# Weight conversions behind attention sums, the 64-token product in another bank, tile 0 loaded by three issuers

## The chip, the core and the metric

The kernel runs on one core of a Trainium2 chip. The metric is the device time of one execution, in microseconds (us); for the kernel before it is the median of three runs. One more execution was recorded by the hardware profiler, and all rows below are of that one.

## What is computed

A decaying attention (no softmax), two matrix layers with a product between them, and a mixture of 8 experts with a cap:

```python
B, H, S, D_ = q.shape                      # 8, 8, 576, 64
scores = 1.0 / np.sqrt(D_) * np.matmul(q, k.transpose(0, 1, 3, 2))
gamma = 1.0 - 2.0 ** (-5.0 - np.arange(H, dtype=np.float32))
rel = pos[:, None] - pos[None, :]
Dmat = np.where(rel >= 0, gamma[:, None, None] ** rel[None, :, :], 0.0)
x = np.matmul(scores * Dmat[None], v)      # -> 4608 tokens of 512
x = ((x @ w1) * (x @ w2) @ w3 @ w_out).astype(np.float32)   # 512 -> 1024 -> 1024 -> 512
logits = x @ w_gate                        # 8 experts
# (token, expert) pairs in falling order of logit: a token goes to the first
# expert that still has room (576 tokens each)
out[mask_e] = np.maximum(x[mask_e] @ w1[e], 0.0) @ w2[e]    # for each expert e
```

The weights w1, w2, w3 and w_out come as 64-bit floats, and the kernel makes 32-bit ones of them on the chip.

## The kernel before

**Attention.** The 4608 tokens are 36 tiles of 128; three tiles are a block of 384 (`TB`), and there are 12 blocks (`NB`). For a tile t, `att_load` loads q, k and v, `att_scale` scales q and k by the decay (L261, VectorE), `att_T` transposes them on TensorE (L274) and ScalarE copies the result out (L276). `att_P` multiplies k by v (L300), `att_QK` q by k (L283), `att_mask` applies the decay mask (L288, VectorE), `att_state` carries the running state on (L310, L312), and `att_AV` multiplies scores and state into two banks (L321, L329). `att_out` adds both: a copy on ScalarE (L337), the sum on VectorE (L343, two halves), its high part on ScalarE (L344) and its low part on GpSimd (L345). High and low part are the x on which the layers work. The generator `attention` issues these in the order seen below and yields a cost after each piece; `T(t + 2)` runs two tiles ahead. A half tile at the start of a sequence (in tiles 0, 4 and so on) has no state before it and so no sum.

**Precision.** Every product of the layers is three matrix products: high x high, high x low, low x high. So each weight is converted from 64 to 32 bits and split, in units of 128 x 512 (`conv`): an absolute value on ScalarE (L196), two one-operand and two two-operand steps on VectorE (L197, L198, L200, L202), the high part on ScalarE (L215), the low part on VectorE (L216). Units 0 to 15 are w1 and w2 by column blocks in turn (unit 8 and 9: w1 and w2 for f = 4), 16 to 23 w_out, from 24 on w3.

**Layers.** `ab(i)` computes (x @ w1) * (x @ w2) for block i: for each of 8 column blocks f one group of 12 products with w1 and one with w2 (L549), a copy by ScalarE (L556) and a multiplication by VectorE (L558). `ab(0)` calls for conversions `LEAD[f]` units ahead of the group at hand. `begin` lays the start: six attention steps merged with the first `LEAD[0]` units, then the first 8 groups of ab(0) merged with `2 * PER` attention steps by the ratio `RAT[1]`, then ab(0) and ab(1) in turn, two groups each (192 products in a row on TensorE), then w3's transposes (`w34_T`, L391) and the rest. w3 and w_out are multiplied into one matrix beforehand. What `merge` gives is a program order; from it a scheduler sets each engine's own queue, and an engine works its queue in order.

**Experts.** For expert e the output products are five groups (L1049): four of 128 tokens and one of 64 (o = 4). Each takes a bank by `mm_bank()`, of which there are two (p4, p5). The 128-token banks are copied out by ScalarE (L1055); the 64-token one needs a copy of one half (L1058) and VectorE's add of the other (L1059). GpSimd scatters the rows to the output (L1060). `HB` are the four half banks in which the first expert layer (L1027) is summed, named py. The order of this stage is planned from modelled times.

**Loads.** SP issues the loads in the order of `ORDER` ("q0 c0 k0 v0 ...": c are constants, w pairs of weight units).

Of the kernel before, what the change touches and what calls it, by code (L numbers as in the profile page):

```python
# [15 lines left out]
TB, NB = 384, 12  # L16
PT = 96
EARLY, LATE0 = 4, 8
LEAD = (3, 4, 4, 4, 4, 4, 4, 4)
LATE = 1.25  # L20
TRIPS = 8
ROUNDS = ((0, 6), (-4, 6), (-4, 6), (-4, 6), (-5, 6))
ORDER = "q0 c0 k0 v0 c1 q1 k1 w0 v1 w1 q2 k2 v2 w2 w3 c2"
Q0 = 10
RAT = (0.75, 0.45, 0.35, 0.36)


def shape_constants():
# [56 lines left out]
def build(ctx, tc, io):  # L85
# [44 lines left out]
    def mm_bank():  # L130
        return MM[nxt("mm", 2)]
# [52 lines left out]
    def conv(u):  # L184
        raw = raws.pop(u)
        lo, hi = raw[:, :, :, 0], raw[:, :, :, 1]
        if u[0] == "w3":
            b = 2048 + 512 * nxt("cv3", 2)
            ta = raw_t[:, b:b + 512]
        else:  # L190
            b = 512 * nxt("cv", 6)
            ta = tmp_t[:, b:b + 512]
        out = ta
        ta = ta.rearrange("p (k f) -> p k f", k=4)
        tb = hi.bitcast(F32)
        A.activation(ta, hi.bitcast(F32), AF.Abs)  # L196
        V.tensor_scalar(ta, ta, HIGH, LOW, op0=OP.min, op1=OP.max)  # L197
        V.tensor_scalar(ta.bitcast(I32), ta.bitcast(I32), 3, 0x3FFFFFF8,  # L198
                        op0=OP.logical_shift_left, op1=OP.bitwise_and)
        V.scalar_tensor_tensor(tb.bitcast(I32), hi, -1073741824, ta.bitcast(I32),  # L200
                               op0=OP.bitwise_and, op1=OP.bitwise_or)
        V.scalar_tensor_tensor(ta.bitcast(I32), lo, 29, tb.bitcast(I32),  # L202
                               op0=OP.logical_shift_right, op1=OP.bitwise_or)
        n, i, j = u
        if n == "w3":
            w3f[u] = out
            return
        hs, ls = SLOT(n)
        if n == "wo":
            hd, ld = hs[:, i, :], ls[:, i, :]  # L210
            fl = out
        else:
            hd, ld = (x[:, :, 128 * i:128 * i + 128] for x in (hs, ls))
            fl = ta
        A.activation(hd, fl, AF.Copy)  # L215
        V.tensor_tensor(ld, fl, hd.bitcast(F32), op=OP.subtract)  # L216
# [97 lines left out]
    def att_AV(t):  # L314
# [9 lines left out]
        for s in range(2):  # L324
            for a in range(2):
                for u, b in QUADS:
# [3 lines left out]
                              buf(t)[2][halves(u), 256 * s + 64 * c:256 * s + 64 * c + 64],  # L330
                              AM[s][halves(u), 64 * c:64 * c + 64], start=True, stop=True, skip_group_check=True)

    def att_out(t):
        j, o = divmod(t, 3)
        us = [u for u in range(2) if (2 * t + u) % 9]
# [2 lines left out]
        for u in range(2):  # L338
            xh, xl = (x[:, :, 128 * o + 64 * u:128 * o + 64 * u + 64] for x in XT[j % 2])
            po = PX[u][:, 0:256]  # L340
            if u in us:
                f = fk[u]
                V.tensor_tensor(f, po.rearrange("p (s a i) -> p s a i", a=2, s=2), f, op=OP.add)  # L343
                A.activation(xh.rearrange("p (s a) i -> p s a i", s=2), f, AF.Copy)  # L344
                G.tensor_tensor(xl.rearrange("p (s a) i -> p s a i", s=2), f,  # L345
                                xh.bitcast(F32).rearrange("p (s a) i -> p s a i", s=2), op=OP.subtract)
# [5 lines left out]
    def attention():  # L352
        def T(t):
            if t < NT:
                att_scale(t)
                att_T(t)
                if t != 2:
                    att_load(t + (3 if t < 2 else 2), (0,))
# [6 lines left out]
        yield 2500  # L365
        for t in range(NT):
            att_AV(t)
            if t + 1 < NT:
                att_P(t + 1)
                att_QK(t + 1)  # L370
                att_mask(t + 1)
            att_out(t)
            yield 2400
            if t + 1 < NT:
                att_state(t + 1)
            T(t + 2)
            att_load(t + 3, (1,))
            if t != 2:
                att_load(t + (3 if t < 2 else 2), (2,))
            yield 1400  # L380
# [633 lines left out]
    def expert(e):  # L1014
# [23 lines left out]
                yield 1500  # L1038
        vh, vl = (slot(i, 8) for i in pairs[(2 * e + 1) % 3])
        for o in (0, 1, 2, 3, 4) if e < E - 1 else (0, 4, 1, 2, 3):  # L1040
            p = mm_bank()
            for f in range(8):
                if o < 4:
                    s = slice(128 * o, 128 * o + 128)
# [65 lines left out]
    def begin():  # L1110
        merge(take(6), conv_some(LEAD[0]), RAT[0])
        a0, a1 = ab(0), ab(1)
        s = take(2 * PER)
        merge(take_from(a0, 8), s, RAT[1])
        drain(s)
        merge(turns(2, a0, take_from(a1, 8)), take(1), RAT[2])
# [16 lines left out]
    for c in ORDER.split():  # L1133
# [5 lines left out]
            load_pair(n)  # L1139
            nload[0] = n + 1  # L1140
        else:
            att_load(n, ("qkv".index(c[0]),))
    G.memset(wg, 0.0)
    SP.dma_start(wg[:, :, 0:8], io["wgate"].rearrange("(c p) e -> p c e", p=128))
    G.memset(WG, 0.0)
# [71 lines left out]
```

## Time and profile before

| what | us |
|---|---|
| median of three runs | 1303.81 (1303.66 to 1306.4) |
| the profiled execution | 1303.38 |
| its span, first to last instruction | 1301.6 |
| TensorE busy | 1256.4 (97%) |
| VectorE / ScalarE / GpSimd busy | 529.0 / 460.8 / 254.4 |

The mean granted clock of TensorE is .984 of its upper level over the span. TensorE is the busiest engine by far, but the share is a mean: the first slices of the span and the last one show less. The other engines are idle for more than half of the time, though not in every stretch. What an engine waits for is read from the waits, from the timeline around one place, and from its queue.

### The profile page before, as it was taken

The page shows a single profiled execution, that of the slowest core. Times are in us where ns is not written, and L with a number is a line of the kernel's source. Part 1 is how long each engine was busy: PE and PEld are TensorE (multiplying, and loading weights), DVE is VectorE, ACT ScalarE, POOL GpSimd, SP SyncE. Part 2 cuts the span into 40 slices and gives each one's busy share as a digit, 9 for nine tenths or more (in the row PEclk, how much of TensorE's full clock was granted, in tenths as well). Part 3 has the DMA queues.
Part 4 walks back from the last instruction along what each step waited for, and adds up shares of the span by engine and source line. Part 5 has one row for each costly group of instructions (what it writes and reads, how often), then busy time and mean ns, then how long its engine had stood idle before and what let it go on. Part 6 is the DMA issues. An engine that isn't in the chain of part 4 may idle for free. (4 is left out here: it accounts for less than half of the span.)

```text
span 1301.6 us, 27200 instructions
## 1 busy us (share of the span) xinstructions
PE 1256.4 (97%) x11416; PEld 1112.1 (85%) x11416; DVE 529.0 (41%) x1298; ACT 460.8 (35%) x989; POOL 254.4 (20%) x238
## 2 busy tenths in 40 slices
PE   5789999999999999999999999989999999999996
PEld 4678988889898989889899777778989989899885
DVE  6797544433231312212212555553533524335220
ACT  4443433343322222212221544333543534435221
POOL 1101211112211120201110734432120211211011
PEclk7799999999999999999999999999999999999999
DMA  9766444422312131424012312163533524435110
GB/s 243 221 163 198 133 131 134 127 64 61 83 34 74 25 83 25 131 87 134 10 49 93 114 45 98 42 190 119 154 121 114 157 67 150 140 96 153 47 39 29
DMA packets 156382, 136.00 MB, mean 104 GB/s; under 512 B 119264, under 2 KB 119520, under 8 KB 155232
## 3 DMA queue, kind: packets, MB, share of 16 engines
q1 hardware_dynamic: 150368, 115.35, 30.3%
q0 software_dynamic: 5888, 18.88, 4.6%
q8 instruction: 91, 1.49, 0.5%
q14 instruction: 35, 0.29, 0.1%
HBM read 107.19 MB, written 27.00 MB: 103 GB/s over the span
## 5 line engine op out<-in xcount | busy, mean ns | idle before, releaser
L549 PE MATMUL p<-x,ws 128*128 128x384 f32 x2304 | 424.1, 339 | 1.7 <-POOL x L345 0.9
L549 PEld LDWEIGHTS p<-x,ws 128*128 128x128 f32 x2304 | 398.2, 189 | 9.8 <-issue 3.9
L1049 PE MATMUL p<-ws,g 128*128 128x512 f32 x864 | 217.9, 394 | 1.9 <-DVE rs L1059 1.4
L1049 PEld LDWEIGHTS p<-ws,g 128*128 128x128 f32 x864 | 156.5, 188 | 31.6 <-DVE rs L1059 1.8
L904 PE MATMUL p<-ws,x 128*128 128x512 f32 x576 | 140.3, 398 | 0.0
L558 DVE TENSOR_TENSOR g<-p,ms 128x384 f32<-128x384 f32 x88 | 48.9, 556 | 183.1 <-PE p L549 180.2
L904 PEld LDWEIGHTS p<-ws,x 128*128 128x128 f32 x576 | 104.8, 189 | 20.6 <-issue 0.7
L941 DVE TENSOR_TENSOR ws<-x,ws 128x512 fp32r<-128x512 f32 x120 | 80.8, 690 | 100.6 <-ACT ws L940 92.7
L261 POOL TENSOR_TENSOR a<-a,cst 128x512 f32<-128x512 f32 x52 | 54.9, 1056 | 302.4 <-DMA a<-q 223.0
L940 ACT ACTIVATE ws<-x 128x512 fp32r<-128x512 f32 x128 | 78.2, 629 | 74.4 <-DMA x<-ew 57.8
L556 ACT ACTIVATE ms<-p 128x384 f32<-128x384 f32 x96 | 47.0, 489 | 151.4 <-PE p L549 149.6
L345 POOL TENSOR_TENSOR x<-a,x 128x256 fp32r<-128x256 f32 x64 | 49.4, 783 | 258.6 <-ACT x L344 258.6
L1060 POOL DMA_INDIRECT out<-rs,idx x40 | 40.0, 999 | 266.6 <-ACT g L1036 147.0
L601 PE MATMUL p<-ws,g 128*128 128x512 f32 x288 | 71.9, 398 | 0.0
L601 PEld LDWEIGHTS p<-ws,g 128*128 128x128 f32 x288 | 52.5, 188 | 13.4 <-issue 2.5
L1027 PE MATMUL p<-a,ws 128*128 128x320 f32 (+1 forms) x384 | 58.9, 301 | 0.5 <-ACT a L1010 0.5
L1036 ACT ACTIVATE g<-py 128x256 fp32r<-128x256 f32 x96 | 31.5, 328 | 75.1 <-PE py L1027 65.1
L1027 PE MATMUL p<-x,ws 128*128 128x320 f32 (+1 forms) x384 | 57.3, 297 | 0.3 <-DVE g L1037 0.3
L1027 PE MATMUL py<-a,ws 128*128 128x320 f32 (+1 forms) x384 | 57.0, 296 | 0.0
L1027 PEld LDWEIGHTS p<-a,ws 128*128 128x128 f32 x384 | 55.1, 193 | 2.1 <-ACT a L1010 0.6
L1027 PE MATMUL py<-x,ws 128*128 128x320 f32 (+1 forms) x384 | 56.4, 296 | 0.3 <-DVE g L1037 0.3
L1027 PEld LDWEIGHTS py<-x,ws 128*128 128x128 f32 x384 | 54.0, 189 | 2.6 <-DVE g L1037 0.7
(191 smaller groups left out, 1484.6 us busy)
## 6 DMA issues: line engine op xcount, KB each, us to landing
x<-ew SPq DMA_DIRECT2D x128, 256.0 KB
y_scratch<-ms SPq DMA_DIRECT2D x36, 256.0 KB
a<-k SPq DMA_DIRECT2D x64, 128.0 KB
ws<-w SPq DMA_DIRECT2D x8, 1024.0 KB
a<-q SPq DMA_DIRECT2D x62, 128.0 KB
a<-v SPq DMA_DIRECT2D x31, 256.0 KB
g_scratch<-g SPq DMA_DIRECT2D x8, 768.0 KB
g<-g_scratch SPq DMA_DIRECT2D x4, 1536.0 KB
```

What stands on the lines that cost most here:

```text
L261: (V if t < Q0 else G).tensor_tensor(xx, xx, tb_[:, :, None].to_broadcast([128, H, DH]), op=OP.mult)
L345: G.tensor_tensor(xl.rearrange("p (s a) i -> p s a i", s=2), f, xh.bitcast(F32).rearrange("p (s a) i -> p s a i", s=2), op=OP.subtract)
L549: PE.matmul(p[:, :TB], w[:, kk, fs], x[:, kk, :], start=(kk == 0 and j == 0), stop=(kk == 3 and j == 2))
L556: A.activation(a, p[:, :TB], AF.Copy)
L558: V.tensor_tensor(g[:, f, :], p[:, :TB], a, op=OP.mult)
L601: PE.matmul(p, x[:, f, ts], w[:, f, :], start=(f == 0 and j == 0), stop=(f == 7 and j == 2))
L904: PE.matmul(p, x[:, f, :], w[:, f, :], start=(f == 0 and j == 0), stop=(f == 7 and j == 2))
L940: A.activation(h, st, AF.Copy)
L941: low.tensor_tensor(lo[:, 512 * u:512 * u + 512], st, h.bitcast(F32), op=OP.subtract)
L1027: PE.matmul(p[:, :n], w[:, kk, fs], x[kk][:, ts], start=(kk == 0 and j == 0), stop=(kk == 3 and j == 2))
L1049: PE.matmul(p, x, w[:, f, :], start=(f == 0 and j == 0), stop=(f == 7 and j == len(ops) - 1))
L1060: st = G.indirect_dma_start(out=out, out_offset=bass.IndirectOffsetOnAxis(ap=idx[:n, 5 * e + o:5 * e + o + 1], axis=0), in_=ob[:n], in_off ...
```

## The change

`conv`: from the fourth unit on, VectorE's first step is issued only after the latest attention sum but one (and not before that of tile 2). `LEAD` falls from 4 to 2, so ab(0) calls for conversions two units ahead; `RAT[1]` rises from .45 to .9. `att_out` of tile 2 comes directly behind its `att_AV`; the scaling of tile 3 and 4 is issued after tile 2's sums, and tile 3's transposes behind that. In the expert stage the 64-token group takes one of the four half banks instead of p4 or p5. k0 is loaded by ScalarE's queue, v0 by GpSimd's, all else by SP's.

```diff
--- before.py
+++ after.py
@@ -1,4 +1,4 @@
-from contextlib import ExitStack
+from contextlib import ExitStack, nullcontext
 import numpy as np
 import concourse.bass as bass
 from concourse import mybir
@@ -16,13 +16,13 @@
 TB, NB = 384, 12
 PT = 96
 EARLY, LATE0 = 4, 8
-LEAD = (3, 4, 4, 4, 4, 4, 4, 4)
+LEAD = (3, 2, 2, 2, 2, 2, 2, 2)
 LATE = 1.25
 TRIPS = 8
 ROUNDS = ((0, 6), (-4, 6), (-4, 6), (-4, 6), (-5, 6))
 ORDER = "q0 c0 k0 v0 c1 q1 k1 w0 v1 w1 q2 k2 v2 w2 w3 c2"
 Q0 = 10
-RAT = (0.75, 0.45, 0.35, 0.36)
+RAT = (0.75, 0.9, 0.35, 0.36)
 
 
 def shape_constants():
@@ -194,7 +194,9 @@
         ta = ta.rearrange("p (k f) -> p k f", k=4)
         tb = hi.bitcast(F32)
         A.activation(ta, hi.bitcast(F32), AF.Abs)
-        V.tensor_scalar(ta, ta, HIGH, LOW, op0=OP.min, op1=OP.max)
+        behind = tc.issue_after(sums[max(2, max(sums) - 1)].ins) if u in units[3:] else nullcontext()
+        with behind:
+            V.tensor_scalar(ta, ta, HIGH, LOW, op0=OP.min, op1=OP.max)
         V.tensor_scalar(ta.bitcast(I32), ta.bitcast(I32), 3, 0x3FFFFFF8,
                         op0=OP.logical_shift_left, op1=OP.bitwise_and)
         V.scalar_tensor_tensor(tb.bitcast(I32), hi, -1073741824, ta.bitcast(I32),
@@ -330,6 +332,8 @@
                               buf(t)[2][halves(u), 256 * s + 64 * c:256 * s + 64 * c + 64],
                               AM[s][halves(u), 64 * c:64 * c + 64], start=True, stop=True, skip_group_check=True)
 
+    sums = {}
+
     def att_out(t):
         j, o = divmod(t, 3)
         us = [u for u in range(2) if (2 * t + u) % 9]
@@ -340,7 +344,7 @@
             po = PX[u][:, 0:256]
             if u in us:
                 f = fk[u]
-                V.tensor_tensor(f, po.rearrange("p (s a i) -> p s a i", a=2, s=2), f, op=OP.add)
+                sums[t] = V.tensor_tensor(f, po.rearrange("p (s a i) -> p s a i", a=2, s=2), f, op=OP.add)
                 A.activation(xh.rearrange("p (s a) i -> p s a i", s=2), f, AF.Copy)
                 G.tensor_tensor(xl.rearrange("p (s a) i -> p s a i", s=2), f,
                                 xh.bitcast(F32).rearrange("p (s a) i -> p s a i", s=2), op=OP.subtract)
@@ -352,7 +356,8 @@
     def attention():
         def T(t):
             if t < NT:
-                att_scale(t)
+                with tc.issue_after(sums[2].ins) if t == 4 else nullcontext():
+                    att_scale(t)
                 att_T(t)
                 if t != 2:
                     att_load(t + (3 if t < 2 else 2), (0,))
@@ -365,15 +370,24 @@
         yield 2500
         for t in range(NT):
             att_AV(t)
+            if t == 2:
+                att_out(t)
+                yield 1400
+                with tc.issue_after(sums[2].ins):
+                    att_scale(3)
+                att_T(3)
+                att_load(5, (0,))
             if t + 1 < NT:
                 att_P(t + 1)
                 att_QK(t + 1)
                 att_mask(t + 1)
-            att_out(t)
+            if t != 2:
+                att_out(t)
             yield 2400
             if t + 1 < NT:
                 att_state(t + 1)
-            T(t + 2)
+            if t != 1:
+                T(t + 2)
             att_load(t + 3, (1,))
             if t != 2:
                 att_load(t + (3 if t < 2 else 2), (2,))
@@ -1038,7 +1052,7 @@
                 yield 1500
         vh, vl = (slot(i, 8) for i in pairs[(2 * e + 1) % 3])
         for o in (0, 1, 2, 3, 4) if e < E - 1 else (0, 4, 1, 2, 3):
-            p = mm_bank()
+            p = mm_bank() if o < 4 else HB[nxt("hb", 4)]
             for f in range(8):
                 if o < 4:
                     s = slice(128 * o, 128 * o + 128)
@@ -1110,7 +1124,7 @@
     def begin():
         merge(take(6), conv_some(LEAD[0]), RAT[0])
         a0, a1 = ab(0), ab(1)
-        s = take(2 * PER)
+        s = take(2 * PER + 1)
         merge(take_from(a0, 8), s, RAT[1])
         drain(s)
         merge(turns(2, a0, take_from(a1, 8)), take(1), RAT[2])
@@ -1139,7 +1153,7 @@
             load_pair(n)
             nload[0] = n + 1
         else:
-            att_load(n, ("qkv".index(c[0]),))
+            att_load(n, ("qkv".index(c[0]),), A if c == "k0" else G if c == "v0" else SP)
     G.memset(wg, 0.0)
     SP.dma_start(wg[:, :, 0:8], io["wgate"].rearrange("(c p) e -> p c e", p=128))
     G.memset(WG, 0.0)

```

What this moves on the engines. In the rows below a name such as a1_10_73 is a region of memory with its place and use, and p0 to p5 and py are banks. The first place is VectorE around the sums of tile 2 (the last two L343 or L347 with p2 and p3 in each piece). In the kernel before:

```order
L200 SCALAR_TENSOR_TENSOR ws5_6_69<-ws5_6_69,g2_16_79 128x4x128
L261 TENSOR_TENSOR a0_9_72<-a0_9_72,cst_63 128x512
L202 SCALAR_TENSOR_TENSOR g2_16_79<-ws5_6_69 128x512
L651 CAST tri16_96<-cst_63 128x128
L288 TENSOR_TENSOR a1_10_73<-py_88,cst_63 128x256 x2
L216 TENSOR_TENSOR ws3_4_67<-g2_16_79,ws2_3_66 128x4x128
L261 TENSOR_TENSOR a0_9_72<-a0_9_72,cst_63 128x512
L343 TENSOR_TENSOR a1_10_73<-p2_84,a1_10_73 128x2x128
L343 TENSOR_TENSOR a1_10_73<-p3_85,a1_10_73 128x2x128
```

ws0 to ws3 are the finished parts of w1 and w2, ws4 and ws5 the raw units, g2 the work region of the conversions. Now (line numbers are higher by 2 to 4):

```order
L290 TENSOR_TENSOR a1_10_73<-py_88,cst_63 128x256 x2
L347 TENSOR_TENSOR a1_10_73<-p2_84,a1_10_73 128x2x128
L347 TENSOR_TENSOR a1_10_73<-p3_85,a1_10_73 128x2x128
L314 TENSOR_TENSOR a2_11_74<-p2_84,a2_11_74 128x256
L314 TENSOR_TENSOR a2_11_74<-p3_85,a2_11_74 128x256
L664 CAST blk16_95<-cst_63 128x128
L665 CAST tri16_96<-cst_63 128x128
L347 TENSOR_TENSOR a1_10_73<-p2_84,a1_10_73 128x2x128
L347 TENSOR_TENSOR a1_10_73<-p3_85,a1_10_73 128x2x128
L199 TENSOR_SCALAR g2_16_79<-g2_16_79 128x512 x2
L200 TENSOR_SCALAR g2_16_79<-g2_16_79 128x512
L263 TENSOR_TENSOR a0_9_72<-a0_9_72,cst_63 128x512
```

The conversions of later units (L200, L202 and L216 before) and three of the scalings (L261) no longer stand ahead of tile 2's sums; they follow behind them.

The second place is VectorE around the sums of tile 5. In the kernel before:

```order
L198 TENSOR_SCALAR g2_16_79<-g2_16_79 128x512
L197 TENSOR_SCALAR g2_16_79<-g2_16_79 128x512
L200 SCALAR_TENSOR_TENSOR ws5_6_69<-ws5_6_69,g2_16_79 128x4x128
L343 TENSOR_TENSOR a1_10_73<-p2_84,a1_10_73 128x2x128
L343 TENSOR_TENSOR a1_10_73<-p3_85,a1_10_73 128x2x128
L312 TENSOR_TENSOR a2_11_74<-p2_84,a2_11_74 128x256
L216 TENSOR_TENSOR ws1_2_65<-g2_16_79,ws0_1_64 128x4x128
L312 TENSOR_TENSOR a2_11_74<-p3_85,a2_11_74 128x256
L558 TENSOR_TENSOR g0_14_77<-p5_87,ms_12_75 128x384
L202 SCALAR_TENSOR_TENSOR g2_16_79<-ws5_6_69 128x512
```

Now:

```order
L204 SCALAR_TENSOR_TENSOR g2_16_79<-ws4_5_68 128x512
L572 TENSOR_TENSOR g0_14_77<-p5_87,ms_12_75 128x384
L347 TENSOR_TENSOR a1_10_73<-p2_84,a1_10_73 128x2x128
L347 TENSOR_TENSOR a1_10_73<-p3_85,a1_10_73 128x2x128
L218 TENSOR_TENSOR ws1_2_65<-g2_16_79,ws0_1_64 128x4x128
L204 SCALAR_TENSOR_TENSOR g2_16_79<-ws4_5_68 128x512
L314 TENSOR_TENSOR a2_11_74<-p2_84,a2_11_74 128x256
L263 TENSOR_TENSOR a0_9_72<-a0_9_72,cst_63 128x512
L218 TENSOR_TENSOR ws3_4_67<-g2_16_79,ws2_3_66 128x4x128
L314 TENSOR_TENSOR a2_11_74<-p3_85,a2_11_74 128x256
L199 TENSOR_SCALAR g2_16_79<-g2_16_79 128x512 x2
L200 TENSOR_SCALAR g2_16_79<-g2_16_79 128x512 x2
```

The last operations of unit 9 (L204 and the second L218) and the first ones of units 10 and 11 (L199, L200) now stand behind tile 5's sums, where units 14 and later stood before.

The third place is the end of ScalarE's queue, the last expert. In the kernel before:

```order
L1036 ACTIVATE g2_37_10508<-py_88 128x256
L1036 ACTIVATE g1_36_10507<-py_88 128x64
L1055 ACTIVATE rs_32_10486<-p4_86 128x512
L1058 ACTIVATE rs_32_10486<-p5_87 64x512
L1055 ACTIVATE rs_32_10486<-p5_87 128x512
```

Now:

```order
L1050 ACTIVATE g2_37_10508<-py_88 128x256
L1050 ACTIVATE g1_36_10507<-py_88 128x64
L1069 ACTIVATE rs_32_10486<-p4_86 128x512
L1072 ACTIVATE rs_32_10486<-py_88 64x512
L1069 ACTIVATE rs_32_10486<-p5_87 128x512
```

The 64-token copy (64x512) now stands between the last two 128-token ones and reads py instead of p5. On TensorE the last sixteen rows are now the 64-token group's, where they were p5's.

On TensorE, tile 0's products of k and v stand ahead of tile 1's transposes, as before; the first product of ab(0) stands directly behind tile 2's last L331, ahead of tile 3's transposes; before, it stood behind the transposes of tiles 3 and 4.

## Rows read from the trace of the kernel before

**Rows 1.** Busy time of each engine in stretches of the span; PEclk is the granted clock.

```profile
core 0: us, PE busy (x) PEld busy (x) DVE busy (x) ACT busy (x) POOL busy (x), PEclk, DMA share, GB/s
0.00:14.40 14.40, 7.56 (x176) 6.50 (x176) 4.01 (x9) 3.83 (x6) 0.66 (x6) 1.00 0.88 224
14.40:45.90 31.50, 16.90 (x352) 13.99 (x352) 30.74 (x66) 14.82 (x28) 2.59 (x3) 0.54 0.73 190
45.90:83.00 37.10, 32.92 (x505) 29.62 (x502) 30.39 (x65) 20.25 (x41) 4.78 (x5) 0.93 0.74 229
83.00:116.80 33.80, 32.90 (x203) 32.33 (x206) 32.49 (x64) 13.79 (x27) 1.85 (x2) 1.00 0.60 183
...
140.00:860.00 720.00, 716.05 (x7149) 624.15 (x7147) 251.79 (x699) 228.26 (x462) 161.79 (x137) 1.00 0.28 82
```

**Rows 2.** TensorE's waits, 0 to 120 us, then from 860 on: total, times, longest.

```profile
PE p L274 <- DVE a L261: 15.7, 6, 5.2
...
PE p L1049 <- DVE rs L1059: 1.4, 1, 1.4
PE p L1049 <- ACT rs L1055: 0.5, 1, 0.5
```

**Rows 3.** Timeline from 30 to 48: start, duration, engine, line, idle before.

```profile
30.01 2.11 PE L329 MATMUL p<-a,g 64*64 64x64 f32 x32
...
38.17 0.68 DVE L216 TENSOR_TENSOR ws<-g,ws 128x512 fp32r<-128x512 f32 x1
38.78 0.68 DVE L261 TENSOR_TENSOR a<-a,cst 128x512 f32<-128x512 f32 x1
...
45.20 0.74 DVE L343 TENSOR_TENSOR a<-p,a 128x256 f32<-128x256 f32 x2
...
47.15 6.45 PE L549 MATMUL p<-x,ws 128*128 128x384 f32 x24
```

**Rows 4.** Timeline from 82 us on, around the sums of tile 5.

```profile
82.26 0.74 DVE L343 TENSOR_TENSOR a<-p,a 128x256 f32<-128x256 f32 x2
...
83.36 1.85 POOL L345 TENSOR_TENSOR x<-a,x 128x256 fp32r<-128x256 f32 x2 [5.99 <-ACT x L344]
...
84.23 0.56 DVE L558 TENSOR_TENSOR g<-p,ms 128x384 f32<-128x384 f32 x1
...
85.27 31.33 PE L549 MATMUL p<-x,ws 128*128 128x384 f32 x179 [0.90 <-POOL x L345]
```

**Rows 5.** Timeline of the first 18 us.

```profile
2.33 0.98 SPq L253 DMA_DIRECT2D a<-k  x2
...
7.74 1.13 PE L300 MATMUL p<-a 64*64 64x64 f32 x32
...
11.17 0.76 DVE L288 TENSOR_TENSOR a<-py,cst 128x256 f32<-128x256 f32 x2 [0.65 <-PE py L283]
...
14.44 1.22 ACT L196 ACTIVATE g<-ws 128x512 f32<-128x512 f32 x2 [1.57 <-DMA ws<-w]
...
17.09 0.69 PE L321 MATMUL py<-a,a 64*64 64x64 f32 x12 [0.84 <-ACT a L337]
```

**Rows 6.** Timeline around tile 7's masks and w3's first transposes.

```profile
118.69 0.76 DVE L288 TENSOR_TENSOR a<-py,cst 128x256 f32<-128x256 f32 x2 [1.77 <-PE py L283]
...
139.96 1.03 PE L391 MATMUL p<-cst,g 128*128 128x128 f32 x8
```

**Rows 7.** Timeline of the last 17 us.

```profile
1285.15 0.59 ACT L1058 ACTIVATE rs<-p 64x512 f32<-64x512 f32 x1
...
1285.78 0.68 DVE L1059 TENSOR_TENSOR rs<-p,rs 64x512 f32<-64x512 f32 x1 [1.45 <-ACT rs L1058]
...
1286.74 0.90 POOL L1060 DMA_INDIRECT out<-rs,idx  x1 [0.43 <-DVE rs L1059]
...
1292.29 0.60 ACT L1055 ACTIVATE rs<-p 128x512 f32<-128x512 f32 x1 [6.54 <-PE p L1049]
1293.16 0.97 POOL L1060 DMA_INDIRECT out<-rs,idx  x1 [5.52 <-ACT rs L1055]
```

## The prediction

> **What bounds the kernel now.** I read the stretches first: from 140 to 860 us TensorE is busy 716.05 of 720 us [rows 1], so nothing that is moved there can pay much; the time to be had lies in the ramp, up to the run of products that begins at 85.27, and in the last 20 us. Between 14.4 and 45.9 us VectorE is busy 30.74 of 31.50 us and TensorE 16.90, at a mean granted clock of .54; between 45.9 and 83.0 VectorE still works 30.39 of 37.10 [rows 1]. The table of waits says for whom: TensorE's largest wait in the first 120 us is for VectorE's scaling of q and k, 15.7 us in six waits [rows 2]. VectorE's queue is filled with weight conversions that nobody needs yet. TensorE's first product of ab(0) comes at 47.15, 1.2 us after tile 2's attention sums (45.20, two rows in .74 us) [rows 3]; those sums stand behind eight units' conversions. The second gate is tile 5's sums at 82.26, behind which GpSimd makes the low part (83.36, 1.85 us for two) and the first product on block 1's x starts at 85.27; from there 179 products run in 31.33 us, .173 us each, without a gap [rows 4].
>
> **First gate: tile 2's sums.** I count VectorE's rows ahead of these sums in the two orders and price them by start-to-start steps: .61 us for a 512-wide row with two tensor operands (38.17 to 38.78), .37 for a narrower or one-operand row (45.20: two in .74) [rows 3]. Before: 35 wide and 35 narrow, 34.3 us. After: 15 and 23, 17.7 us; three units are ahead instead of eight. VectorE thus has some 13.7 us left to do from 14.4 on (4.01 were done by then [rows 1]), and ceases to set this gate: 14.4 + 13.7 = 28.1. What sets it then is the chain of tiles 1 and 2: scaling, transposes, masks, states, and the products with v. Before, the last of these ran 30.01 to 32.12 [rows 3], already ahead of most of the conversions. Two changes of its pace nearly cancel. ScalarE's copy for tile 0, which the next states wait for (17.09 [rows 5]), now stands behind unit 0's high part and two more absolute values, about 3 us later; against that one or two conversions less stand between the links on VectorE, 2.2 to 2.4 us. I take 32.8 for the end of tile 2's products and 33.6 for its sums, with bounds 30.5 (ScalarE's delay hidden) and 37.0 (nothing won on VectorE). First product: 33.6 + 1.2 = 34.8 instead of 47.15.
>
> **Second gate: tile 5's sums.** The conversions that were moved are not removed. Between the sums of tile 2 and tile 5 stand now 27 wide, 32 narrow and 4 multiplications (.56 each [rows 4]), 30.6 us; before 26, 33 and 4, 30.3 us, which took 37.1 us. The same work in the same kind of stretch: 33.6 + 37.1 = 70.7. The floor is TensorE's own work there, 32.92 us [rows 1], which would give 66.5; VectorE's 30.6 is lower. Behind these sums stands something new, the end of unit 9, which had been finished long before: four wide rows and a narrow one, 2.8 us, so the second group of ab(0)'s f = 4 starts at 73.5, and block 1's first product 12 x .173 = 2.1 us later, at 75.6 against 85.27: 9.7 us earlier. GpSimd's low part (2.2 us after the sums, as before) is covered by these 2.1 and 2.8 us; if unit 9 were already there it would cap the gain at 11.7.
>
> **Is it carried on?** Eight units' work now stands behind tile 5's sums. The next ones: unit 10 is done 8.2 us behind the sums, at 78.9, and due at 75.6 + 24 x .173 = 79.8; 11 at 79.9, due at 81.8; 12 and later have 3 us and more. The last check is w3's first unit, which TensorE transposes at 139.96 [rows 6], so now due at 130.3. In front of it stand, behind tile 5's sums, 52 wide rows, 44 narrow ones and 10 multiplications: 53.6 us. VectorE ran 32.49 of 33.80 us (96%) from 83.0 to 116.8 and 82% from 45.9 to 83.0 [rows 1]. At 96% they end at 70.7 + 55.8 = 126.5 and the gain stands; at 82% at 70.7 + 65.4 = 136.1, 5.8 us late. It is the kind of work of the first stretch (conversions beside long product runs), so I take 96%. Tile 7's masks, at 118.69 after all conversions before [rows 6], now stand amid them, 36 us behind the sums at that density, about 107: no wait for TensorE, which needs them by 109, but with only 2 us to spare.
>
> **Loads.** Three of SP's issues go away, k0's two (.98 us [rows 5]) and v0's one, at the same price 1.47, so all that follows is issued up to 1.47 us earlier. But the DMA engines are busy .88 of the first 14.4 us [rows 1], and the first conversion waited for the data of w (14.44, released by DMA [rows 5]), not for its issue. I take 0, with bounds 0 and -1.47. The Trainium skill says the same more strongly (DMA: Bandwidth & Descriptors, section Issuing engines are not separate DMA queues): all issuers share 16 engines, and spreading the issue saves only the sequencer's time. By it the sum is the one below; if all of the 1.47 us of issue were won, it would be 1293.1.
>
> **Expert stage.** The 64-token product gets a bank of its own, so two TensorE waits for the pair of banks fall in the last expert: 1.4 us for VectorE's add and .5 for ScalarE's copy [rows 2]. But the planner answers by putting that product last: TensorE's last sixteen rows are now its, and ScalarE's last three evictions are p4, the 64 rows, p5. Before, from TensorE's end: .04 + .60 + .27 + .97 (copy and scatter of 128 tokens) = 1.88 us to the last issue. After: copy of 64 rows .59, add .68, scatter .90, then the last scatter .97, with gaps of .04, .04, .28, .27 = 3.77, all by the rows of the last product and of the 64-token one [rows 7]. So +1.9 against -1.9, and I allow .5 for one new wait on the shared bank (the size of the smaller wait). Net +.5; bounds -1.9 and +1.9.
>
> **Sum.** 1303.38 (the profiled execution; span 1301.6 and 1.8 around it) - 9.7 + .5 = 1294.2. That execution lies .4 under the median of the three, so 1294.6 is my time.
>
> **The rivals.**
> *Smaller gain.* VectorE is less dense behind tile 5's sums, since each unit's first operation may start only behind the sums: at the 82% of the earlier stretch w3's first transposes come 5.8 us late, and the time is 1300.4. For it: one unit's chain runs VectorE, ScalarE, VectorE, and fewer units are now in flight at a time. Against: 96% in the stretch of the same kind. Times 1298 to 1301.2.
> *Larger gain.* The chain is not delayed by ScalarE (30.5) and the second stretch runs at TensorE's floor (32.9 us): up to 3.1 + 4.2 us more, less where unit 10 is not ready by its new due time; 1287.3 to 1290.5.
> *The loads of tile 0 become the gate: slower.* v0 is issued by GpSimd, whose price is not in the trace for this shape. The nearest row is the scatter of 128 rows, .97 us of GpSimd [rows 7]; v0 has 1024 pieces (128 tokens, 8 heads), so 1 to 8 us, and nearest by the count of instructions (one) is 1. The products of tile 0's k and v stood at 7.74 and its masks were through at 11.9 [rows 5]; they stand second on TensorE, ahead of tile 1's transposes, so a late v0 holds all of tile 1. Since the first conversion starts only at 14.44, a landing at 10.2 costs nothing; later each us goes to the end. Issue at 1, price 1 to 8 and the landing give 3 to 11, so .8 us of the gain is lost at most. The change turns slower from a landing at about 22: 10.2 + 9.2 + 2.6; at 24 the time is 1308.4. The Trainium skill warns of this (SBUF — State Buffer, section SBUF: two separate sides): GpSimd cannot write its descriptors while some VectorE instructions hold the shared port. No run here shows it yet; before 14.4 VectorE is busy 4.01 of 14.4 us [rows 1], so the lock would have few instructions to work with.
> *The order does not bite: same.* The first products come 12 us earlier but the scaling of tiles 3 and 4, which now waits for tile 2's sums, holds tile 5 as late as before (sums(5) above 80). Then only the net of the expert stage is left, 1303 to 1304.
>
> **How the numbers follow.** What a measurement of this kernel can tell from no change is about .2%, 2.6 us: 1301.2 to 1306.4 is the same. Forecast .52 (its own range 1290.5 to 1298); smaller gain .20; larger gain .10; same .10; slower .08. The first three are faster: .82. The range 1288.0 to 1302.0 leaves out the slower case, most of the same one, and the far part of the larger gain, about .2.
>
> **What would show it.** Right: tile 2's sums near 33.6 and the first product at 34.8; tile 5's sums near 70.7; block 1's first product at 75.6 followed by a run without gaps; the clock at its upper level within some 5 us of the first product (before, .54 until 45.9 and .93 in the next stretch [rows 1]); w3's transposes at 130; from TensorE's last row to the last scatter 3.8 us instead of 1.9. Wrong: a wait of TensorE for v0 above 4 us at the start; a hole in the run of products behind 75; TensorE waiting at w3's first transposes; tile 5's sums after 78.

## The result: slower, and not where the prediction looked

The changed kernel takes 1319.11 us (median of four, 1318.41 to 1319.63) against 1303.82; the ratio is 1.0109, 95% interval 1.0093 to 1.0126. The forecast was 1294.6 with a range up to 1302.0. Its profiled execution has a span of 1317.3 us against 1301.6.

The start did what was forecast up to the run of products on block 1. Timeline of the changed kernel, first 110 us (start, duration, engine, line, in brackets the idle time before and its releaser):

```profile
12.45 1.22 ACT L196 ACTIVATE g<-ws 128x512 f32<-128x512 f32 x2 [0.20 <-DMA ws<-w]
...
31.23 0.76 DVE L347 TENSOR_TENSOR a<-p,a 128x256 f32<-128x256 f32 x2 [0.58 <-ACT a L341]
...
32.48 1.01 PE L563 MATMUL p<-x,ws 128*128 128x384 f32 x2 [1.56 <-ACT x L348]
...
70.00 0.74 DVE L347 TENSOR_TENSOR a<-p,a 128x256 f32<-128x256 f32 x2
...
73.72 33.92 PE L563 MATMUL p<-x,ws 128*128 128x384 f32 x192
```

Tile 2's sums stand at 31.2 (before 45.20 [rows 3]), tile 5's at 70.0 (before 82.26 [rows 4]); block 1's first product is 12 products into the run of 192, at 75.8 (before 85.27), and the run ends at 107.6 where it ended at 116.6. Thus 9.0 us are won at 107 us. All but 2.0 of them are gone by 144: w3's first transposes come at 132.2 instead of 139.96 [rows 6], but the first product with w3 at 143.8 instead of 145.7. Even these 2.0 do not stand out: in x1_bank below, whose start is the old one, that product comes at 143.8 too. At 860 us both kernels start the experts at the same moment. Their first and last rows on TensorE in the kernel before, and their first row in the changed one (its last one is in the tail below):

```profile
860.61 0.80 PE L1027 MATMUL p<-a,ws 128*128 128x256 f32 x2 [0.47 <-ACT a L1010]
...
1291.86 0.39 PE L1049 MATMUL p<-ws,h 128*128 128x512 f32 x1
```

```profile
860.46 0.79 PE L1041 MATMUL p<-a,ws 128*128 128x256 f32 x2 [0.47 <-ACT a L1024]
```

The loss is made in the experts. From their first product to the last, TensorE takes 431.6 us before and 443.2 after; from its end to the end of the last scatter's issue 1.9 us before [rows 7] and 6.1 after. Together 15.8, against a span that grew by 15.7. Of the 11.6 us inside the stage, 6.8 are time in which TensorE has nothing to do (2.5 us before, 9.3 now). In the other 4.7 the same 2584 recorded products take longer (429.2 and 433.9 us); the mean granted clock of the stage fell from 1.00 to .99. TensorE's waits in the experts, changed kernel (total, times, longest), where the kernel before had 1.9 us for two banks [rows 2]:

```profile
PE p L1063 <- ACT g L1050: 5.1, 7, 1.8
PE p L1063 <- DVE g L1051: 2.5, 2, 2.2
...
PE p L1041 <- DVE g L1051: 1.1, 1, 1.1
PE p L1063 <- ACT rs L1069: 0.5, 1, 0.5
```

L1063 is the second layer's product, L1050 and L1051 the split of the first layer's result into high and low part. The waits for the banks by VectorE are gone, as forecast, and 8.7 us of waits for the splits stand in their place. Timeline of the changed kernel at two of them:

```profile
1099.50 1.27 ACT L954 ACTIVATE ws<-x 128x512 fp32r<-128x512 f32 x2 [3.02 <-DMA x<-ew]
...
1102.64 1.19 PE L1063 MATMUL p<-ws,g 128*128 128x512 f32 x4 [2.21 <-DVE g L1051]
...
1199.45 1.60 PE L1041 MATMUL py<-a,ws 128*128 128x256 f32 x12
...
1202.96 1.29 ACT L954 ACTIVATE ws<-x 128x512 fp32r<-128x512 f32 x2 [2.54 <-DMA x<-ew]
...
1204.16 0.36 ACT L1050 ACTIVATE g<-py 128x256 fp32r<-128x256 f32 x1
...
1204.58 1.20 PE L1063 MATMUL p<-ws,g 128*128 128x512 f32 x4 [1.77 <-ACT g L1050]
```

The reader should see what is ahead of the split on ScalarE: copies of the next expert's weights (L954), which themselves wait 2.5 to 3.0 us for the transfer. ScalarE works in order. At 1204 the split that TensorE needs thus waits for a weight that nobody needs yet: its sum in py was through at 1201.05, and it comes at 1204.16, right behind the copies. At 1100 the wait for the transfer was over before the sum was there (1100.13); what stood ahead there were the late copies themselves, two before the first part of the split (1100.79) and one more before the second (1101.86). ScalarE waited for these transfers in the kernel before too, at 53.5 us in sum and now 53.7; but there TensorE waited only .6 us for a split.

The tail, changed kernel:

```profile
1299.89 3.79 PE L1063 MATMUL py<-ws,g 128*128 128x512 f32 x16
...
1301.01 0.97 POOL L1074 DMA_INDIRECT out<-rs,idx  x1 [14.04 <-ACT rs L1069]
1303.71 0.59 ACT L1072 ACTIVATE rs<-py 64x512 f32<-64x512 f32 x1 [2.98 <-PE py L1063]
1304.34 0.68 DVE L1073 TENSOR_TENSOR rs<-py,rs 64x512 f32<-64x512 f32 x1 [5.01 <-ACT rs L1072]
1305.30 0.90 POOL L1074 DMA_INDIRECT out<-rs,idx  x1 [3.32 <-DVE rs L1073]
1307.96 0.60 ACT L1069 ACTIVATE rs<-p 128x512 f32<-128x512 f32 x1 [3.65 <-DMA out<-rs,idx]
1308.83 0.97 POOL L1074 DMA_INDIRECT out<-rs,idx  x1 [2.63 <-ACT rs L1069]
```

The last copy waits 3.65 us, not for TensorE but for the scatter issued at 1301.01 to land: there are two output buffers, and three groups now end close together.

### The profile page after: what moved, and what is told of

The parts are those of the page before. It is cut to its first block, busy times and chain, and to the rows that moved or that the text cites. A ratio compares the mean times of both kernels' runs of the same rounds, so it can differ in the third digit from the quotient of the medians.

```text
span 1317.3 us, 27178 instructions
## 1 busy us (share of the span) xinstructions
PE 1265.8 (96%) x11416; PEld 1116.4 (85%) x11416; DVE 537.3 (41%) x1298; ACT 459.1 (35%) x989; POOL 257.8 (20%) x239
## 5 line engine op out<-in xcount | busy, mean ns | idle before, releaser
L563 PE MATMUL p<-x,ws 128*128 128x384 f32 x2304 | 429.7, 342 | 2.9 <-ACT x L348 1.6
L1063 PE MATMUL p<-ws,g 128*128 128x512 f32 x800 | 208.2, 397 | 8.1 <-ACT g L1050 5.1
L1063 PEld LDWEIGHTS p<-ws,g 128*128 128x128 f32 x800 | 144.1, 189 | 35.6 <-ACT g L1050 7.6
L572 DVE TENSOR_TENSOR g<-p,ms 128x384 f32<-128x384 f32 x88 | 48.9, 556 | 177.1 <-PE p L563 175.3
L263 POOL TENSOR_TENSOR a<-a,cst 128x512 f32<-128x512 f32 x52 | 56.0, 1078 | 299.9 <-DMA a<-q 248.4
L954 ACT ACTIVATE ws<-x 128x512 fp32r<-128x512 f32 x128 | 78.7, 630 | 77.9 <-DMA x<-ew 58.1
L615 PE MATMUL p<-ws,g 128*128 128x512 f32 x288 | 71.9, 398 | 0.0
L1051 DVE SCALAR_TENSOR_TENSOR g<-py,g 128x256 fp32r<-128x256 f32 (+1 forms) x88 | 30.8, 350 | 100.4 <-ACT g L1050 100.3
L1050 ACT ACTIVATE g<-py 128x256 fp32r<-128x256 f32 x96 | 31.4, 327 | 113.4 <-PE py L1041 100.5
L615 PEld LDWEIGHTS p<-ws,g 128*128 128x128 f32 x288 | 52.5, 188 | 13.3 <-issue 2.5
L1041 PEld LDWEIGHTS py<-a,ws 128*128 128x128 f32 x384 | 55.7, 194 | 2.2
```

The lines of the kernel that those rows point to most:

```text
L263: (V if t < Q0 else G).tensor_tensor(xx, xx, tb_[:, :, None].to_broadcast([128, H, DH]), op=OP.mult)
L563: PE.matmul(p[:, :TB], w[:, kk, fs], x[:, kk, :], start=(kk == 0 and j == 0), stop=(kk == 3 and j == 2))
L572: V.tensor_tensor(g[:, f, :], p[:, :TB], a, op=OP.mult)
L615: PE.matmul(p, x[:, f, ts], w[:, f, :], start=(f == 0 and j == 0), stop=(f == 7 and j == 2))
L954: A.activation(h, st, AF.Copy)
L1041: PE.matmul(p[:, :n], w[:, kk, fs], x[kk][:, ts], start=(kk == 0 and j == 0), stop=(kk == 3 and j == 2))
```

## Experiments

All times are medians, with the ratio to the kernel before in the same job and its 95% interval.

### Which part makes the loss

Theory A: the bank. Rival B: the moved start hands the experts another timing.

**x1_bank**, the bank alone on the kernel before:

```diff
-            p = mm_bank()
+            p = mm_bank() if o < 4 else HB[nxt("hb", 4)]
```

> The kernel before with the 64-token product in a half bank and nothing else. Theory A (the bank makes the whole loss: in the changed kernel TensorE's work in the expert stage lasts 443.2 us instead of 431.7, and 6.1 us instead of 1.9 lie between its end and the last scatter's issue): about 1303.8 + 11.5 + 4.2 = 1319.5. Rival B (the moved start hands the experts another timing, and the bank alone is worth the +.5 us of the prediction): 1302 to 1306.

Measured 1318.49, 1.0109 (1.0087 to 1.0131): the whole loss. **x2_nobank** is the changed kernel with that line as it was:

> The changed kernel with the 64-token product back in the pair of banks: the start and the loads alone. Theory A: the 2.0 us that are left of the start's gain at 848 us, less what the gathers ahead of the experts take back: 1301.5 to 1304. Rival B: the loss stays, above 1310. Rival C (the start would gain its 9.7 us if the experts did not disturb): 1294 to 1296.

1302.76, .9986 (.9976 to .9995): theory A holds, and of the start's gain .14% is left, 1.8 us. **x3_ramp**, in which SP issues all loads as well, and **x4_loads**, the three issuers alone on the kernel before:

> As the one before it, and all loads issued by SP again: the moved conversions and sums alone. If the three issuers gave the start its first conversion 2.0 us earlier (12.45 instead of 14.44), tile 2's sums come some 2 us later than 31.2, near 33.6 as forecast, and the time is 0 to 2 us above the kernel with three issuers. If they gave nothing, the two agree within 1 us.

> The kernel before with k0 and v0 loaded by other queues and nothing else. If the loads help: the first conversion near 12.5 and the run of products on block 1 some 2 us earlier than 85.27, time 1301 to 1303. If VectorE's queue of conversions sets the pace anyway, or the data arrives no earlier: 1303 to 1304.5. The slower rival of the prediction (v0 late by GpSimd): above 1306.

x3: 1307.13, 1.0022 (1.0009 to 1.0034). x4: 1304.07, .9999 (.9986 to 1.0012). Alone the issuers are worth nothing, as forecast. Beside the moved start they are worth .36%, but not for the reason expected, a later first gate: without them tile 2's sums come at 30.5, earlier still, since ScalarE's copy for tile 0 stands at 15.47 instead of 18.76. The two profiles don't show it either: x3's profiled execution took 1304.25 us, one of its shortest, and x2's 1307.51, its longest. The mean granted clock doesn't settle it: seven of x3's other nine executions had .981 to .983 and x2's .984 to .987, but the one of x3 at .991 took 1306.98, as long as those. What the .36% comes from stays open.

### What the bank does to the experts

Theory G: the half bank held by the 64 tokens is missing from the first layer. Rival H: with p4 and p5 free, the planner opens two 128-token sums at once. On the kernel before, **y3_tr** gives the 64 tokens a bank of the transposes (`TR[nxt("tr", 2)]`), so the first layer keeps its four halves. **y4_first7** uses the half bank except in the last expert.

> The kernel before with the 64-token product in one of the two banks of the transposes (p0, p1), so the four half banks of the first expert layer are left alone. Theory G (the loss of the bank change comes from the half bank that is held open for the 64 tokens, so that the first layer has fewer of them): the expert stage stays at 431 to 434 us, time 1303 to 1308. Rival H (any bank that frees p4 and p5 lets the planner open both 128-token sums at once, which take up each fresh block of the first layer at once and leave nothing to cover ScalarE's and VectorE's split): 1312 to 1320, with TensorE's waits for ScalarE's and VectorE's split of 5 us or more.

> The kernel before with the half bank in the first seven experts alone; the last one as before. If the loss is spread (a few us in the seven, and the rest in the last expert with its wait for the output buffer): the end's 4.2 us and the last expert's waits of some 3 us are gone, 1309 to 1313. If nearly all of it is the last expert: 1304 to 1307. If it is all in the seven: 1316 to 1319.

y3: 1323.64, 1.0156 (1.0139 to 1.0174), with 11.3 us of waits for ScalarE's split in five; so the half bank is not needed for a loss of this kind, though this kernel takes a bank from the transposes instead, whose own price no run shows. y4: 1318.62, 1.0110 (1.0093 to 1.0127). Its profile has the 4.2 us of the tail back (9.3 us from TensorE's end to the span's end, x1 13.6), and the same 444.8 us of experts as x1 (444.7). So the loss inside the stage is made in the first seven experts. The times of the two agree all the same: in these executions y4's experts started 2.5 us later (862.7 and 860.2), and x1's took 1.7 us more than its median.

**z2_serial** lets one output sum be open at a time, with the half bank; **z4_serial_mm** the same with the pair:

```diff
-                    PE.matmul(p, x, w[:, f, :], start=...)
+                    with tc.issue_after(last[-1].ins) if f == j == 0 and last else nullcontext():
+                        m = PE.matmul(p, x, w[:, f, :], start=...)
...
+            last.append(m)
```

> The kernel before with the half bank for the 64 tokens in all experts, and each output sum's first product placed behind the sum before it, so that only one is open at a time. Theory H (the loss comes from two 128-token sums that are open at once and take up each fresh block at once): TensorE's waits for ScalarE's and VectorE's split fall from 8 us to under 3, the expert stage returns to 431 to 435 us, time 1302 to 1307. Theory G (the half bank itself is missing from the first layer): the stage stays near 444 us, 1314 to 1320.

> The kernel before with its pair of banks, and each output sum placed behind the one before it. If the one sum at a time is in itself good (the 1.9 us of waits for banks in the last expert and the fine turns between p4 and p5 go): 1300 to 1303. If it only removes cover (the next expert's first layer must fill every gap): 1304 to 1309.

z2: 1312.56, 1.0064 (1.0042 to 1.0087); z4: 1306.03, 1.0014 (1.0003 to 1.0025). One sum at a time gives back 6 of the 14 us, which neither theory said. With it, the half bank still costs 6.5 us more than the pair.

**n1_plain** and **n2_plain_hb** leave the planning of the stage out (`nullcontext()` for the planned block), with the pair and with the half bank:

> The kernel before with its pair of banks, and the expert stage in plain program order instead of the order planned from modelled times. It is the base for the next one: each output sum runs nearly in one piece (24 products in a row). Expected a few us above the kernel before, 1304 to 1312, since fewer turns cover the splits.

> As the one before it in plain order, with the half bank for the 64 tokens. Theory I (the loss of 14 us is that of the order which the planner makes for the freed banks, not of the bank): within 3 us of the plain order with the pair of banks, on either side. Theory G (the half bank that the first layer lacks): 7 us or more above it.

n1: 1313.25, 1.0064 (1.0047 to 1.0081); n2: 1319.27, 1.0116 (1.0100 to 1.0133). The half bank costs 6 us here too, short of the 7 us or more of theory G and beyond the 3 of theory I. The waits of the first layer's products for VectorE's split, that is, for a half bank to come free, show 4.0 of it, 7.8 us against 3.8 (two of the four half banks are named p in the trace, two py). n1, then n2:

```profile
PE py L1027 <- DVE g L1037: 2.2, 4, 0.8
PE p L1027 <- DVE g L1037: 1.6, 5, 0.6
```

```profile
PE py L1027 <- DVE g L1037: 7.4, 7, 1.9
...
PE p L1027 <- DVE g L1037: 0.4, 2, 0.2
```

And the planned order is worth 8.5 us with the pair (1304.75 in the same job), which is what a new order puts at stake.

**w1_noload** and **w2_noload_hb** leave out the transfers of the experts' weights but for the first three blocks (the arithmetic stays, on what lies in the staging buffers), with the pair and with the half bank, to test whether ScalarE's waits for them make the rest:

> The kernel before without the loads of the experts' weights: only the first three blocks are read, all later conversions take what lies in the three staging buffers (all else of the work stays). It is the base for the next one: TensorE's work is the same and was not waiting for weights, 1300 to 1305.

> As the one before it, with the half bank for the 64 tokens. Theory J (in ScalarE's queue the copies of the next expert's weights stand ahead of the split that TensorE needs next, and wait 1 to 3 us for the weights' transfer; with the half bank TensorE has no cover left for that): without the transfers the waits inside the stage vanish and what is left is the tail's 4 us and the last expert's short waits of .5 us, together 3 to 7 us above the base. Theory K (the order itself costs it, by its shorter runs and the missing half bank): 11 us or more above the base.

w1: 1316.39, 1.0091 (1.0061 to 1.0120); w2: 1317.73, 1.0107 (1.0082 to 1.0133). w2 is 1.3 us above w1, under the 3 to 7 of theory J and far under the 11 of theory K. TensorE's waits for splits inside w2's experts:

```profile
PE p L1053 <- ACT g L1040: 4.1, 6, 1.2
```

Here the base missed its expectation by 11 us: without the transfers the planner makes another order, in which the experts start at 866.1 and last 438.6 us instead of 431.6 with the pair. With the half bank they last 436.6, 8.0 us less than in x1 (444.7) and 2.0 less than in w1; only the tail is longer, by 4.2. The waits for VectorE's split are gone and the longest for ScalarE's is 1.2 us instead of 2.4. That would put the transfers' cost to the half bank's order at some 8 us, but since the order changed with them, it isn't shown that they alone do; and the pair's stage is 7 us longer in its new order. How the 13 us inside the stage are shared between the missing half bank (6.0 and 6.5 us in two comparisons), the two open sums and the transfers behind which the splits stand stays open: the parts overlap, and each kernel had its own order.

### Where the start's gain went

Theory D: w3's units come late, TensorE waits and its clock falls. **y1_w34_6** spreads w3's transposes thinner (`W34RATE = 0.6`); **y2_gate16** frees the units from 16 on of the gate; both are the changed kernel with the pair of banks, as x2:

```diff
-        behind = tc.issue_after(...) if u in units[3:] else nullcontext()
+        behind = tc.issue_after(...) if u in units[3:16] else nullcontext()
```

> The changed kernel with the pair of banks, and w3's transposes spread thinner over TensorE's queue (W34RATE .6 instead of 1.0), so that their units are due later. Theory D (the 9 us that the start has won at 107 us are lost by 145 us because w3's units come late, TensorE waits for them and its clock falls): the waits for w3's units vanish, the clock stays at 1.00 from 120 to 150, and the time is 3 to 7 us under the kernel with rate 1.0 (1302.8), 1296 to 1300. Rival E (VectorE's total work is late anyway and the wait turns up at the next user): within 1.5 us of 1302.8.

> The changed kernel with the pair of banks, and the sums ahead of conversions only for units 3 to 15; the units of w_out and w3 are free of them. Theory D with the gate as the cause of the lateness: w3's first unit is ready 2 us or more earlier than 135.2 and the time 2 to 5 us under 1302.8. Rival F (it is late because tile 7's masks stand amid the conversions on VectorE and wait there for TensorE's long run to end, 2.9 us at 109.5, and because GpSimd slows VectorE's rows): 1301.5 to 1304.

y1: 1303.55, 1.0004 (.9992 to 1.0016), rival E: the wait turned up at a multiplication of ab(1), TensorE waiting 6.6 us for VectorE's L572. y2: 1300.15, .9968 (.9957 to .9979), so the gate on w_out and w3 cost 2.6 us (x2: 1302.76). But w3's first transposes come at 135.6, no earlier than x2's 135.2. The wait for them is gone, yet from the long run's end to the first product with w3 TensorE waits 3.8 us as against 4.1, now at attention products; the mean granted clock there is .95 instead of .90. So theory D is right in the time and not in the reason. **g10** gates only units 3 to 9 (`units[3:10]`), **g10_again** is the same once more, **g0_nogate** has no gate (`()`), **g10_sp** the gate on 3 to 9 with all loads on SP. All keep the earlier sums of tile 2, the lead of two and the pair of banks.

> The changed kernel with the pair of banks, and the sums ahead of conversions for units 3 to 9 alone. If the gate costs the later units their start at every sum, as units 16 on have shown (1300.2 instead of 1302.8): tile 5's sums a few us later than 70, the run of products later by the same, but w3's units earlier than 135.6, and 1298 to 1300.5. If freeing units 10 to 15 only puts conversions ahead of tile 5's sums again: the run on block 1 starts after 78, and the time is 1301 to 1304.

> The same kernel as the gate on units 3 to 9, for a closer comparison with the two beside it: 1298 to 1301, .2 to .5% under the kernel before.

> As the one before it without any gate on the conversions: the shorter lead, the earlier sums of tile 2 and the loads remain. If the shorter lead does the work and the gate only orders what would come so anyway: within 1.5 us of the gated one. If units 3 to 9 crowd in ahead of the sums again: tile 2's sums after 35, the run on block 1 after 79, 1301 to 1304.

> As the first of the three, with all loads of tile 0 issued by SP. With the moved start the three issuers were worth .36% (1302.8 against 1307.1), with the old start nothing (1304.1 against 1304.1). If that holds with the gate on units 3 to 9: 2 to 5 us above it. If it was chance of those runs: within 1 us.

g10: 1298.70, .9956 (.9938 to .9973), and again 1299.80, .9964 (.9953 to .9976). g10_sp: 1302.35, .9985 (.9975 to .9995), so here too the three issuers go with .2%, unexplained. **g0_nogate: 1294.80, .9922 (.9907 to .9936)**, faster than both kernels of this case by .8% and 1.8%. Its expectation was wrong: without the gate tile 2's sums come at 32.6 and not after 35, tile 5's at 73.5; so the shorter lead and the order of tile 2 do the work (no run takes these two apart), and the gate costs 8 us (1302.8 against 1294.8). Of these, 5.0 come from units 3 to 9 (g10_again, in the same job); the stretches below are of the full gate, and why those units alone cost so much isn't shown. Stretches around w3's first units (TensorE, its weight loads, VectorE, ScalarE and GpSimd busy; granted clock; transfers), changed kernel first, then g0:

```profile
107.00:120.00 13.00, 13.00 (x298) 11.73 (x297) 9.75 (x18) 4.79 (x10) 4.39 (x4) 1.00 0.64 184
120.00:132.00 12.00, 10.05 (x163) 9.25 (x162) 11.93 (x21) 6.19 (x12) 4.47 (x4) 0.86 0.51 132
132.00:146.00 14.00, 11.46 (x53) 10.22 (x53) 10.79 (x22) 5.97 (x13) 2.72 (x3) 0.76 0.64 203
```

```profile
107.00:120.00 13.00, 12.29 (x295) 11.02 (x294) 11.04 (x24) 5.73 (x11) 2.42 (x3) 1.00 0.84 247
120.00:132.00 12.00, 12.00 (x200) 11.34 (x200) 4.45 (x12) 5.25 (x12) 6.50 (x8) 1.00 0.63 149
132.00:146.00 14.00, 14.00 (x85) 12.03 (x86) 8.40 (x16) 5.33 (x10) 1.50 (x2) 1.00 0.62 204
```

In the changed kernel VectorE is idle 3.25 of 13 us just behind the long run, and full in the 12 us that follow, in which TensorE waits; in g0 it is busy in 4.45 of these 12. The rows of the changed kernel show how:

```profile
109.50 0.76 DVE L290 TENSOR_TENSOR a<-py,cst 128x256 f32<-128x256 f32 x2 [2.94 <-PE py L285]
...
114.15 1.33 POOL L263 TENSOR_TENSOR a<-a,cst 128x512 f32<-128x512 f32 x1 [1.46 <-DMA a<-k]
114.50 1.27 DVE L200 TENSOR_SCALAR g<-g 128x512 int32<-128x512 int32 x1
...
132.25 0.66 PE L405 MATMUL p<-cst,g 128*128 128x128 f32 x4 [0.16 <-DVE g L204]
134.58 0.66 PE L405 MATMUL p<-cst,g 128*128 128x128 f32 x4 [1.67 <-DVE g L204]
...
135.94 7.24 PE L563 MATMUL p<-x,ws 128*128 128x384 f32 x24 [0.71 <-DVE g L572]
```

Tile 7's masks (L290) now stand ahead of conversions, and VectorE waits 2.94 us there for TensorE's run to end. The conversions behind them fall into a stretch where GpSimd scales tiles: L200 takes 1.27 us beside GpSimd's L263 and .42 alone, and the five L204 from 107 to 132 take 957 ns in the mean, in g0 three take 684. That is what the Trainium skill states (SBUF — State Buffer, section SBUF: two separate sides): VectorE and GpSimd share a pair of ports, and when a row of VectorE that runs in a two-port mode or reads two SBUF inputs meets one of GpSimd, whichever starts first has the pair for its whole instruction and the other stands. The trace agrees here, with .85 us lost on that one row. No run takes GpSimd's rows away, so how much of the lateness they make isn't shown. Then TensorE waits, and its granted clock is .86 and .76 in the mean: at the lower of its two levels (1.2 of 2.4 GHz) from 125.0 to 128.4 and from 135.3 to 142.1, else at the upper one. 24 products take 7.24 us at 135.94 where g0 has 4.41 at 131.86:

```profile
131.07 1.03 PE L405 MATMUL p<-cst,g 128*128 128x128 f32 x8
131.86 4.41 PE L563 MATMUL p<-x,ws 128*128 128x384 f32 x24
...
136.84 0.95 PE L421 MATMUL p<-ws,g 128*128 128x512 f32 x3
```

From the end of the long run to the first product with w3 the changed kernel takes 36.2 us and the kernel before 29.2. Of the 7.0 us, 2.1 are more waits (4.4 and 2.4), and 4.9 are nearly the same work taking longer, 3.6 of them 96 products of the layers; an estimate by the clock alone, 9.6 us of work at the lower level that would take half as long at the upper one, gives 4.8.

## Why the prediction failed, point by point

- **First gate** (33.6, first product 34.8): 31.2 and 32.5, inside the bounds. ScalarE's delay was 2.1 us and not 3 (copy at 18.76 instead of 16.66), and fewer conversions gave 3.3 where 2.2 to 2.4 were counted (the last products of tile 2 end at 30.9, before 32.1).
- **Second gate** (70.7; block 1's first product at 75.6): 70.0 and 75.8. The mechanism was right, with unit 9 as the gate of the second group; that the numbers meet so closely is in part luck, since the gate came 2.4 us early and the stretch behind it took 38.8 us instead of 37.1. (A product is .175 us by the row used, 31.33 by 179, and not .173; nothing hangs on it.)
- **Is it carried on?** This step failed. VectorE was to run at 96% to w3's first unit at 126.5. It ran at 99.8% to 104 us and at 84% after, and the unit came at 132.2 (VectorE's busy times in these two stretches of the changed kernel are 33.24 and 23.74 us):

```profile
70.70:104.00 33.30, 33.12 (x198) 32.07 (x197) 33.24 (x66) 16.68 (x32) 2.75 (x2) 1.00 0.60 195
104.00:132.20 28.20, 26.14 (x477) 23.98 (x476) 23.74 (x42) 12.27 (x24) 8.86 (x8) 0.94 0.61 171
```

Its rows took 57.0 us where 53.6 were counted, and it stood idle for 4.5 where 96% leaves 2.2. The step asked whether TensorE waits for tile 7's masks, and had 2 us to spare; it did not ask whether VectorE waits there for TensorE, with all conversions behind it, and it priced VectorE's rows without GpSimd beside them. The rival "smaller gain" names this end, w3's units 5.8 us late and 1300.4; x2, the start and the loads without the bank, has 1302.8. The rival had no term for the lower clock, which went with most of the loss (4.9 of 7.0 us).
- **Loads** (0): x4 confirms the time, but not the reason: the first conversion did come earlier, at 12.01 in x4 instead of 14.44, and little of it reached the run on block 1 (84.83 instead of 85.27). v0 on GpSimd cost 1.08 us of GpSimd, the low end of 1 to 8. The rival of late loads was wrong: tile 0's products of k and v wait for no v, at 8.27.
- **Expert stage** (+.5): this step failed too. It was +11.6 in the stage and +4.2 in the tail, and this decided the sign. The prediction saw that the planner answers with another order, but read only its last rows. It priced the banks' waits that go, and not what TensorE would stand before next in the seven experts ahead: the splits, one half bank less, ScalarE's copies that wait for transfers. The tail's 3.8 became 6.1, since three groups share two output buffers and the scatter's landing was left out. The slower case had .08, for another reason.
- **Sum.** A gain of the size of the start's 9.7 us was there to be had, with another order behind it: g0_nogate, which keeps the shorter lead, tile 2's order and the loads, and drops gate and bank, runs at 1294.8. That this stands beside the forecast 1294.6 is luck: the gate, by which the forecast worked, cost 8 us.

## What to carry to other kernels

A wait that is removed from a stage whose order a planner sets is not the price of the change: compare the whole new order with the old, and look on every in-order queue for operations on far transfers that now stand ahead of what the bound engine needs next. When work is moved behind a gate, ask on the moved engine too whether it will stand there for others, and what runs beside it then. Test each part of such a change alone; here two of its parts, the bank and the gate, cost more than the .8% that the rest was worth.

## What the runs showed of the hardware

- A scatter of 128 rows held its output buffer until it had landed: issued at 1301.01, and the copy that waited for the buffer began at 1307.96.
- One load of 128 x 8 pieces on GpSimd's queue took 1.08 us of GpSimd (v0, at 1.29 in the changed kernel).
- In the changed kernel TensorE stood .79 and 1.16 us at 122.7 and 124.3, and the granted clock was .50 from 125.0 to 128.4; it stood 1.67 us up to 134.6, and the clock was .50 again from 135.3 to 142.1. It was not so in each execution: the profiled one of x3_ramp had 1.00 from 120 to 132 with the same 10.05 us of work, and .76 from 132.
